# Splitting the per-head scaling of linear-attention tiles between ScalarE, VectorE and GpSimd, with one routing step moved in TensorE's order

## The chip, the cores and the metric

The kernel runs on one core of a Trainium2 chip, as one launch. The metric is device time in microseconds of that launch. A core has TensorE (PE, matmuls into PSUM), VectorE (DVE), ScalarE (ACT), GpSimd (POOL), SyncE (SP, here a queue that issues DMAs), and 16 DMA engines. Each engine works through its own instructions in their order; semaphores make them wait for each other.

## The reference, cut to what matters

Linear attention over 4 batches of 576 rows, 8 heads of 64, is followed by an RMS norm of each head, and by two mixture-of-experts layers of 8 experts over the 2304 rows of 512.

```python
kv  = einsum('bhsd,bhse->bhde', k, v)
out = einsum('bhsd,bhde->bhse', q, kv)
rms = sqrt(mean(out * out, axis=-1, keepdims=True) + 1e-06)
x   = out / rms * g_norm                 # (B,H,S,64), then rows of 512
# layer 1: rows with x @ w_skip > 0 go to expert argmax(x @ w_gate): x + gate * relu(x @ w1[e]) @ w2[e]
# layer 2: every row goes to its expert, up to a capacity: gate * relu(x @ w1[e]) @ w2[e]
```

## The kernel before, in words

The 2304 rows are 18 tiles of 128; tile numbers t0 to t17 below count them. Batch 0 fills t0 to t3 and half of t4, batch 1 ends with t8, batch 2 with half of t13.

**Attention, batch by batch.** `emit_kv` sums k·v of a batch on PE in five chunks (c0 to c4) into the PSUM tile `acc`, and ACT copies the two blocks of each head pair to `vk`. `emit_kvT` (written T) runs two filler matmuls on zeros into the PSUM tile `lg` (`warm`), transposes `vk` into the same `lg`, multiplies `vk` by the gate weights into `acc`, and ACT copies both to `kvbd`, which holds 128 columns of kv and 34 of gate weights for each head pair.

**One tile.** `emit_products(i)` multiplies q by `kvbd` into one of three PSUM tiles `ops` (pool `apo`). `emit_tile(i)` then norms it. ACT squares (`sq`), DVE sums by head (`ss`), ACT takes the root (`rm`), DVE the reciprocal (`ri`). DVE scales the 34 gate columns (`lh`) and sums them over heads to 17 logits (`Lall`). ACT copies `ops` to `og` in one instruction, POOL multiplies `og` by g_norm and then by `ri` into the row tile `xr`; 16 logits are copied behind the row, and SP writes `xr` to the table `xcat` in DRAM. For t15 alone (`G_DVE`) DVE multiplies `ops` by g_norm instead of ACT's copy and POOL's first multiply. From t16 on (`LPOOL`) POOL copies the logits. An `ops` tile can be written again when all its readers have read it.

**Routing.** After t8 the logits of the first nine tiles pick experts on DVE (`choose1`: `sel`, `oa_mx`, `oa_eq`, `oh`), a scan gives counts (`C`), PE sums them over partitions into `lg` (`R`, lines 178 and 183), and DVE makes ranks (line 196 on), one-hot matrices `As` and a table `Bt`, which PE turns into row numbers (line 796). With them POOL gathers the first 128 rows of the fullest expert (`rows`), which starts its first-layer product early (`t1`, `l1`, `l2`, lines 574, 592, 626) while the other nine tiles are ranked in the same way. The copies of that early expert's transposed rows, `xT` on line 576 and 580, are ACT's.

**Order.** PE's order is written by hand (`manual_schedule`): `ATT_SEQ` for the attention, where `t0` to `t4` are the tiles of a batch, `c0` to `c4` the chunks of the next one, `r` and `R` the two halves of the ranking, `e`, `E`, `m0`, `w` the early expert, and `EARLY_SEQ` behind it. The order on ACT, DVE and POOL is set by a scheduler from the order of the code and its own costs.

```python
ATT_SEQ = [..., "r t0 q c0 c1 t1 t2 c2 c3 R c4 t3 T", "e m0 m1 E w w p0 p1 t2 w w t3 t4"]
EARLY_SEQ = "v7 t v3 h0 h1 R h2 h3 T y0 y1 y2 y3"
```

In `EARLY_SEQ`, `v7` and `v3` are fillers, `t` the transposes of the gathered rows, `h` the first and `y` the second product of the early expert, `R` and `T` the ranking of the last nine tiles.

Of the kernel before, what the change touches and what calls it, by code (L numbers as in the profile page):

```python
# [7 lines left out]
F32 = mybir.dt.float32  # L8
# [21 lines left out]
CAP1 = [240, 176, 164, 156, 148, 144, 140, 136]  # L30
CAP2 = [384, 352, 320, 308, 300, 292, 280, 272]
EPS_G = 1e-9
LPOOL = 16
G_DVE = (15,)
EARLY_SEQ = "v7 t v3 h0 h1 R h2 h3 T y0 y1 y2 y3"
ATT_SEQ = ["t0 c0 c1 t1 t2 c2 c3 c4 t3 T", "t0 c0 c1 t1 t2 c2 c3 c4 t3 T t4", "r t0 q c0 c1 t1 t2 c2 c3 R c4 t3 T", "e m0 m1 E w w p0 p1 t2 w w t3 t4"]
KV_COL = True
SPLIT1 = (1, 2, 3, 4, 5)
AS_POOL = 0
WARM_T, LATE = 2, 100000  # L40
# [7 lines left out]
def moe_kernel(ctx: ExitStack, tc: tile.TileContext, qT, kk, vv, aux, w1a, w2a, w1b, w2b, capacity, out):  # L48
    nc = tc.nc
# [47 lines left out]
    for m, caps in ((1, CAP1), (2, CAP2)):  # L97
        t = cst.tile([1, E], F32, name=f"capc{m}")
# [23 lines left out]
    grep = au[:, 68:68 + HD]  # L122
# [13 lines left out]
    Lall = cst.tile([128, NT, 17], F32, name="Lall")  # L136
# [155 lines left out]
    m1 = first_mix.enter_context(tc.tile_pool(name="m1", bufs=1, side="right"))  # L292
# [339 lines left out]

    att = ExitStack()
    aq, asp0, asp, axp = (att.enter_context(tc.tile_pool(name=n, bufs=b)) for n, b in (("aq", 3), ("as0", 1), ("as", 3), ("ax", 12)))
    akv = att.enter_context(tc.tile_pool(name="akv", bufs=2))
    apo = att.enter_context(tc.tile_pool(name="apo", bufs=3, space=PSUM))
    with att:
        warm(p1u.tile([128, 512], F32, name="acc"), 10)
        kvbd_all, vk_all = [], []
        for i in range(2):  # L640
            kvbd_all.append(asp0.tile([128, 4, 162], F32, name=f"kvbd{i}"))
            t = asp0.tile([128, 4, 128], F32, name=f"vk{i}")
# [61 lines left out]
        def emit_kvT(b):  # L704

            vk, kb = vk_all[b % 2], kvbd_all[b % 2]
            tp = p1u.tile([128, 4, 128], F32, name="lg")
            warm(tp, WARM_T)
            for hp in range(4):
                nc.tensor.transpose(tp[:, hp, :], vk[:, hp, :], ident)  # L710
            wp = p1u.tile([128, 4, 128], F32, name="acc")
            for hp in range(4):
                nc.tensor.matmul(wp[:, hp, 0:34], lhsT=vk[:, hp, :], rhs=gw[:, hp, :], start=True, stop=True)
            with tc.high_priority():
                nc.scalar.copy(out=kb[:, :, 0:128], in_=tp)
                nc.scalar.copy(out=kb[:, :, 128:162], in_=wp[:, :, 0:34])
# [3 lines left out]
        def emit_products(i):  # L720
            t0 = i * 128
            segs = []
            o = 0
            while o < 128:
                b, s = divmod(t0 + o, S)
                n = min(128 - o, S - s)
                segs.append((o, n, b, s))
                o += n
            ps = apo.tile([128, 4, 256], F32, name="ops")
            for (o, n, b, s) in segs:  # L730
                for hp in range(4):
                    nc.tensor.matmul(ps[o:o + n, hp, 0:162], lhsT=qt[b][:, hp, s:s + n],
                                     rhs=kvbd_all[b % 2][:, hp, :], start=True, stop=True)
            PS[i] = ps

        def emit_tile(i):
            if i not in PS:
                emit_products(i)
            ps, t0 = PS[i], i * 128
            sq = asp.tile([128, 4, 128], F32, name="sq")  # L740
            nc.scalar.activation(out=sq, in_=ps[:, :, 0:128], func=AF.Square)
            ss = asp.tile([128, H], F32, name="ss")
            nc.vector.tensor_reduce(out=ss, in_=sq.rearrange("p c (h d) -> p (c h) d", h=2), axis=AX.X, op=ALU.add)
            og = asp.tile([128, H, HD], F32, name="og")
            o4, og4 = ps[:, :, 0:128].rearrange("p c (h d) -> p c h d", h=2), og.rearrange("p (c h) d -> p c h d", c=4)
            if i in G_DVE:
                nc.vector.tensor_tensor(out=og4, in0=o4, in1=grep.unsqueeze(1).unsqueeze(1).to_broadcast([128, 4, 2, HD]), op=ALU.mult)
            else:
                nc.scalar.copy(out=og4, in_=o4)
            rm = asp.tile([128, H], F32, name="rm")  # L750
            nc.scalar.activation(out=rm, in_=ss, func=AF.Sqrt, bias=eps6, scale=1.0 / HD)
            ri = asp.tile([128, H], F32, name="ri")
            nc.vector.reciprocal(out=ri, in_=rm)
            xr = axp.tile([128, ROW], F32, name="xr")
            r4 = ri.rearrange("p (c h) -> p c h", c=4).unsqueeze(3)
            lh = asp.tile([128, 4, 2, 17], F32, name="lh")
            nc.vector.tensor_tensor(out=lh, in0=ps[:, :, 128:162].rearrange("p c (h n) -> p c h n", h=2),
                                    in1=r4.to_broadcast([128, 4, 2, 17]), op=ALU.mult)
            nc.vector.tensor_reduce(out=Lall[:, i, :], in_=lh.rearrange("p c h n -> p n (c h)"), axis=AX.X, op=ALU.add)
            (nc.gpsimd.tensor_copy if i >= LPOOL else nc.scalar.copy)(out=xr[:, D:ROW], in_=Lall[:, i, 0:16])  # L760
            steps = [] if i in G_DVE else [(og, grep.unsqueeze(1))]
            steps.append((xr[:, 0:D].rearrange("p (h d) -> p h d", h=H), ri.unsqueeze(2)))
            for k, (dst, by) in enumerate(steps):
                ins = nc.gpsimd.tensor_tensor(out=dst, in0=og, in1=by.to_broadcast([128, H, HD]), op=ALU.mult)
                if "gather" in ahead and k == 0:
                    behind(ins, ahead["gather"])
            nc.sync.dma_start(out=xcat[t0:t0 + 128, :], in_=xr)

        with tc.manual_schedule(engines={mybir.EngineType.PE}):
            emit_kv(0, range(5))  # L770
            emit_kvT(0)
            def late(f):
                p = tc.cur_priority
# [34 lines left out]
            for b in range(B):  # L808
                t = list(range((b * S) // 128 if b else 0, ((b + 1) * S) // 128))
                for u in ATT_SEQ[b].split():  # L810
                    if u == "T":
                        emit_kvT(b + 1)
                    elif u == "r":
                        gen = choose_part(routed, t[0], bump1)
                        routed = t[0]
                        late(lambda: next(gen))
                    elif u == "R":
                        late(lambda: run(gen))
                        ranked = routed
# [50 lines left out]
    with first_mix:  # L870
# [11 lines left out]
        for i in range(2):  # L882
            t = cst.tile([128, NB1, E], BF16, name=f"o2_{i}")
# [541 lines left out]
```

## Time and profile before

| | |
|---|---|
| median of 3 runs | 502.59 us (501.24 to 503.12) |
| profiled execution: its own time | 502.82 us |
| its span, first to last instruction | 501.2 us |
| PE busy | 477.4 us (95%) |
| DVE busy | 303.7 us (61%) |
| ACT busy | 205.8 us (41%) |
| POOL busy | 143.3 us (29%) |

The span is 1.6 us shorter than the time of the same execution. Shares of busy time are means over attention (up to about 68 us), the early expert (to about 88 us) and the two expert layers (the rest), which differ in what limits them.

### The profile page before, as it was taken

The page shows a single profiled execution, that of the slowest core. Times are in us where ns is not written, and L with a number is a line of the kernel's source. Part 1 is how long each engine was busy: PE and PEld are TensorE (multiplying, and loading weights), DVE is VectorE, ACT ScalarE, POOL GpSimd, SP SyncE. Part 2 cuts the span into 40 slices and gives each one's busy share as a digit, 9 for nine tenths or more (in the row PEclk, how much of TensorE's full clock was granted, in tenths as well). Part 3 has the DMA queues.
Part 4 walks back from the last instruction along what each step waited for, and adds up shares of the span by engine and source line. Part 5 has one row for each costly group of instructions (what it writes and reads, how often), then busy time and mean ns, then how long its engine had stood idle before and what let it go on. Part 6 is the DMA issues. An engine that isn't in the chain of part 4 may idle for free.

```text
span 501.2 us, 10243 instructions
## 1 busy us (share of the span) xinstructions
PE 477.4 (95%) x3829; PEld 454.8 (91%) x3829; DVE 303.7 (61%) x945; ACT 205.8 (41%) x524; POOL 143.3 (29%) x179
## 2 busy tenths in 40 slices
PE   6998869799999999999999999999999999999995
PEld 3897759699999999999999799999999999999985
DVE  3167977276677665455775485664756576575711
ACT  1376541254433523113432364444555455554400
POOL 5288583101131121212125230130603215040201
PEclk8699798899999999999999999999999999999999
DMA  8999594689787776457317995465546646400001
GB/s 245 362 366 321 194 341 128 225 316 343 268 291 251 240 279 212 155 190 276 126 45 253 417 338 173 132 236 169 188 175 233 216 139 231 162 36 1 36 22 40
DMA packets 24617, 104.90 MB, mean 209 GB/s; under 512 B 3609, under 2 KB 4761, under 8 KB 15984
## 3 DMA queue, kind: packets, MB, share of 16 engines
q1 hardware_dynamic: 17264, 77.75, 44.9%
q0 software_dynamic: 7008, 26.35, 14.9%
q8 instruction: 32, 0.52, 0.4%
q14 instruction: 25, 0.20, 0.1%
q10 hardware_dynamic: 288, 0.07, 0.1%
HBM read 92.15 MB, written 12.76 MB: 209 GB/s over the span
## 4 chain that ended last, share of the span: by engine, by line
PE 75%; DVE 3%; DMA 2%; issue 1%; ACT 0%; POOL 0%; POOLq 0%; ACTq 0%
PE hp L592 14%; PE yp L1089 7%; PE yp L1091 7%; PE yp L1090 7%; PE hp L1089 6%; PE hp L1090 6%; PE hp L1091 6%; PE yp L616 6%; PE yp L626 5%; PE yp L617 2%; PE yt L1318 2%; PE tp L1274 2%; DMA wraw<-in_w1b 2%; PE tp L1011 1%; PE tp L574 1%
## 5 line engine op out<-in xcount | busy, mean ns | idle before, releaser
L979 ACT CAST whi<-wraw 128x512 fp32r<-128x512 f32 x152 | 86.1, 619 | 73.3 <-PE yp L1090 30.1
L980 DVE TENSOR_TENSOR wlo<-wraw,whi 128x512 fp32r<-128x512 f32 x152 | 97.4, 684 | 27.4 <-ACT whi L979 26.3
L592 PE MATMUL hp<-xT,wraw 128*128 128x128 f32 (+8 forms) x576 | 81.3, 300 | 3.2 <-issue 3.0
L339 POOL DMA_INDIRECT rows<-xcat,gi x40 | 42.1, 1051 | 141.5 <-ACT ex L348 88.4
L592 PEld LDWEIGHTS hp<-xT,wraw 128*128 128x128 f32 x576 | 76.6, 198 | 5.6 <-issue 4.9
L1089 PE MATMUL hp<-xh,whi 128*128 128x256 f32 (+7 forms) x256 | 78.9, 308 | 0.3 <-DVE hl L1109 0.3
L1091 PE MATMUL hp<-xh,wlo 128*128 128x256 f32 (+7 forms) x256 | 76.7, 299 | 0.0
L1090 PE MATMUL hp<-xl,whi 128*128 128x256 f32 (+7 forms) x256 | 76.6, 299 | 0.0
L1089 PE MATMUL yp<-hh,whi 128*128 128x320 f32 (+5 forms) x192 | 58.8, 306 | 0.0
L1091 PE MATMUL yp<-hh,wlo 128*128 128x320 f32 (+5 forms) x192 | 57.2, 298 | 0.0
L1090 PE MATMUL yp<-hl,whi 128*128 128x320 f32 (+5 forms) x192 | 57.2, 298 | 0.0
L1308 POOL DMA_INDIRECT out<-ot,toki x24 | 32.3, 1348 | 84.4 <-DVE su L352 39.4
L1089 PEld LDWEIGHTS hp<-xh,whi 128*128 128x128 f32 x256 | 48.2, 188 | 1.1 <-DVE hl L1109 0.8
L1090 PEld LDWEIGHTS hp<-xl,whi 128*128 128x128 f32 x256 | 48.3, 189 | 0.0
L1091 PEld LDWEIGHTS hp<-xh,wlo 128*128 128x128 f32 x256 | 48.3, 189 | 0.0
L1027 POOL DMA_INDIRECT xcat<-rows,toki x16 | 16.4, 1028 | 94.3 <-DVE mxt L297 91.8
L616 PE MATMUL yp<-hT,whi 128*128 128x352 f32 (+4 forms) x160 | 43.1, 351 | 0.0
L1108 ACT ACTIVATE hh<-hp 128x320 fp32r<-128x320 f32 (+8 forms) x64 | 27.2, 429 | 32.8 <-PE hp L1091 28.0
L1109 DVE SCALAR_TENSOR_TENSOR hl<-hp,hh 128x320 fp32r<-128x320 f32 (+8 forms) x64 | 30.0, 476 | 14.3 <-ACT hh L1108 13.1
L617 PE MATMUL yp<-hT,wlo 128*128 128x176 f32 (+4 forms) x160 | 37.7, 235 | 0.0
L1090 PEld LDWEIGHTS yp<-hl,whi 128*128 128x128 f32 x192 | 36.2, 188 | 0.0
L1089 PEld LDWEIGHTS yp<-hh,whi 128*128 128x128 f32 x192 | 36.1, 188 | 0.0
(255 smaller groups left out, 870.4 us busy)
## 6 DMA issues: line engine op xcount, KB each, us to landing
wraw<-in_w1a SPq DMA_DIRECT2D x14, 1024.0 KB
wraw<-in_w2a SPq DMA_DIRECT2D x14, 1024.0 KB
wraw<-in_w1b SPq DMA_DIRECT2D x14, 1024.0 KB
wraw<-in_w2b SPq DMA_DIRECT2D x14, 1024.0 KB
xcat<-xr SPq DMA_DIRECT2D x18, 264.0 KB
q<-in_q SPq DMA_DIRECT2D x3, 1152.0 KB
wraw<-in_k SPq DMA_DIRECT2D x6, 512.0 KB
wraw<-in_v SPq DMA_DIRECT2D x6, 512.0 KB
```

Source lines behind the costliest of these rows:

```text
L339: return nc.gpsimd.indirect_dma_start(out=rows[:n], out_offset=None, in_=xcat[0:source], in_offset=bass.IndirectOffsetOnAxis(ap=gi[:n], ax ...
L592: nc.tensor.matmul(hp[:, ff, :], lhsT=wv[:, fc % 4, k, :], rhs=XT[j][:, k, c0:c1], start=(k == 0), stop=(k == 3))
L616: nc.tensor.matmul(yp, lhsT=wh[:, fc, :], rhs=HT[j][:, fc], start=(fc == 0), stop=False, skip_group_check=True)
L617: nc.tensor.matmul(yp[:, 0, :], lhsT=wl[:, fc, :], rhs=HT[j][:, fc, 0, :], start=False, stop=(fc == 7), skip_group_check=True)
L979: nc.scalar.copy(out=hi[:, cs], in_=raw[:, cs])
L980: ins = nc.vector.tensor_tensor(out=lo[:, cs], in0=raw[:, cs], in1=hi[:, cs].bitcast(F32), op=ALU.subtract)
L1089: nc.tensor.matmul(ps, lhsT=wh, rhs=xh, start=first, stop=False)
L1090: nc.tensor.matmul(ps, lhsT=wh, rhs=xl, start=False, stop=False)
L1091: nc.tensor.matmul(ps, lhsT=wl, rhs=xh, start=False, stop=last)
L1108: ea = nc.scalar.activation(out=hh[:, fs, cs], in_=hp, func=AF.Relu)
L1109: ev = nc.vector.scalar_tensor_tensor(out=hl[:, fs, cs], in0=hp, scalar=0.0, in1=hh[:, fs, cs].bitcast(F32), op0=ALU.max, op1=ALU.subtract)
L1308: st = nc.gpsimd.indirect_dma_start(out=out, out_offset=bass.IndirectOffsetOnAxis(ap=r2["toki"][:nn, j, bi:bi + 1], axis=0), in_=ot[:nn], ...
```

## The change

- Each tile has a kind (`KINDS`). In a **B** tile (t0, t1, t2, t4, t5, t6, t8, t9, t11, t12, t14, t15) ACT scales each of the 8 heads by its column of `ri`, in 8 instructions of 128x64 from `ops` to `og`, in place of one copy of 128x512, and POOL multiplies once, by g_norm. In a **D** tile (t3, t7, t10, t13, t16) DVE multiplies `ops` by g_norm and POOL multiplies once, by `ri`; ACT copies nothing. In the one **A** tile (t17) DVE multiplies by g_norm, ACT scales the 8 heads, and POOL does nothing.
- `LPOOL = 99`: ACT copies the logits of all tiles.
- In batch 2's sequence `R` comes behind `c4 t3` and not ahead of them.
- `emit_kvT` runs its two fillers for batch 0 alone, so 3 pairs go.
- `og` has a pool of 5 buffers of its own, where it had 3. `sq`, `lh` and the g_norm product are written with the even heads first; sizes stay.

```diff
-LPOOL = 16
-G_DVE = (15,)
+LPOOL = 99
+KINDS = "BBBDBBBDBBDBBDBBDA"
...
-"r t0 q c0 c1 t1 t2 c2 c3 R c4 t3 T"
+"r t0 q c0 c1 t1 t2 c2 c3 c4 t3 R T"
...
+    aog = att.enter_context(tc.tile_pool(name="aog", bufs=5))
...
-            warm(tp, WARM_T)
+            if b == 0:
+                warm(tp, WARM_T)
...
-            og = asp.tile([128, H, HD], F32, name="og")
-            if i in G_DVE:
-                nc.vector.tensor_tensor(out=og4, in0=o4, in1=grep.unsqueeze(1).unsqueeze(1).to_broadcast([128, 4, 2, HD]), op=ALU.mult)
-            else:
-                nc.scalar.copy(out=og4, in_=o4)
...
+            og = aog.tile([128, H, HD], F32, name="og")
+            kind = KINDS[i]
+            if kind in "DA":
+
+                nc.vector.tensor_tensor(out=byparity(og), in0=o4, in1=grep.unsqueeze(1).unsqueeze(1).to_broadcast([128, 2, 4, HD]), op=ALU.mult)
+            if kind in "BA":
+
+                for h in range(H):
+                    src, dst = (ps[:, h // 2, (h % 2) * HD:(h % 2) * HD + HD], og) if kind == "B" else (og[:, h, :], x3)
+                    nc.scalar.activation(out=dst[:, h, :], in_=src, func=AF.Copy, scale=ri[:, h:h + 1])
...
-            steps = [] if i in G_DVE else [(og, grep.unsqueeze(1))]
-            steps.append((xr[:, 0:D].rearrange("p (h d) -> p h d", h=H), ri.unsqueeze(2)))
...
+            steps = {"P": [(og, grep.unsqueeze(1)), (x3, ri.unsqueeze(2))], "D": [(x3, ri.unsqueeze(2))],
+                     "B": [(x3, grep.unsqueeze(1))], "A": []}[kind]
```

Three places show what the scheduler and the hand-written order make of it. First ACT around t3 and t4, before: `sq_436` is t3's square and `sq_477` t4's, each with its copy to `og` next to it.

```order
L741 ACTIVATE sq_436<-ops_431 128x512
L749 COPY og_440<-ops_431 128x512
L715 COPY kvbd1_199<-lg_454 128x4x128
L716 COPY kvbd1_199<-acc_461 128x4x34
L751 ACTIVATE rm_442<-ss_438,eps6_123 128x8
L741 ACTIVATE sq_477<-ops_468 128x512
L760 COPY xr_446<-Lall_146 128x16
L749 COPY og_481<-ops_468 128x512
L751 ACTIVATE rm_483<-ss_479,eps6_123 128x8
```

The same place on ACT with the change; `sq_457`, `rm_461` and `xr_466` are t3's (a D tile), `sq_495` and `og_503` t4's, `sq_541` is t5's.

```order
L746 ACTIVATE sq_457<-ops_452 128x2x4x64
L746 ACTIVATE sq_495<-ops_486 128x2x4x64
L750 ACTIVATE rm_461<-ss_459,eps6_123 128x8
L750 ACTIVATE rm_499<-ss_497,eps6_123 128x8
L769 COPY xr_466<-Lall_146 128x16
L768 ACTIVATE og_503<-ops_486,ri_501 128x64 x8
L769 COPY xr_504<-Lall_146 128x16
L746 ACTIVATE sq_541<-ops_536 128x2x4x64
```

t4's reads of `ops` now stand behind both roots and behind the copy of t3's logits, where before they stood next to its square; the next squares stand behind t4's eight heads.

Second, ACT at the end of the attention. Before, from t17's square (`sq_984`) to the copies of the early expert's rows:

```order
L741 ACTIVATE sq_984<-ops_979 128x512
L760 COPY xr_945<-Lall_146 128x16
L751 ACTIVATE rm_967<-ss_963,eps6_123 128x8
L749 COPY og_988<-ops_979 128x512
L751 ACTIVATE rm_990<-ss_986,eps6_123 128x8
L576 COPY xT1_1039<-tp1_1040 128x2x128
L580 COPY xT1_1039<-tp1_1044 128x2x128
```

With the change, from t15's heads (`og_1002`) on; `sq_1049` is t17's square, `rm_1031` and `xr_1036` are t16's.

```order
L768 ACTIVATE og_1002<-ops_989,ri_1000 128x64 x8
L769 COPY xr_1003<-Lall_146 128x16
L750 ACTIVATE rm_1031<-ss_1029,eps6_123 128x8
L746 ACTIVATE sq_1049<-ops_1044 128x2x4x64
L769 COPY xr_1036<-Lall_146 128x16
L750 ACTIVATE rm_1053<-ss_1051,eps6_123 128x8
L768 ACTIVATE xr_1058<-og_1057,ri_1055 128x64 x8
L769 COPY xr_1058<-Lall_146 128x16
L576 COPY xT1_1111<-tp1_1112 128x2x128
L580 COPY xT1_1111<-tp1_1116 128x2x128
```

The copies of the early expert's rows stood behind t17's root and now stand behind its eight heads and its logits too.

Third, PE at the end of batch 2, with the change, from the last chunks on:

```order
L699 MATMUL acc<-wraw 64x64 x16
L699 MATMUL acc<-k_252,v_253 64x64 x8
L734 MATMUL ops<-kvbd_199,q_248 128x162 x4
L178 LDWEIGHTS ones
L178 MATMUL lg<-C_0_695,ones 128x72
L183 LDWEIGHTS ntri
L183 MATMUL lg<-oh_0_685,ntri 128x72
L712 MATMUL lg<-ident,vk_203 128x128 x4
```

The ranks' product into `lg` stood ahead of `c4` and t12's product and is now behind them, right ahead of the transposes, which write the same `lg` (before, a product and two fillers lay between).

## Rows read from the trace of the kernel before

**Rows 1.** The page's first line, and windows: stretch, length, then busy time by engine.

```profile
span 501.2 us, 10243 instructions
17.50:50.00 32.50, 30.28 (x379) 27.85 (x380) 19.71 (x55) 20.62 (x57) 24.77 (x23) 0.92 1.03 344
50.00:75.00 25.00, 19.39 (x127) 16.29 (x125) 21.43 (x68) 12.61 (x32) 17.12 (x19) 0.88 0.73 266
```

**Rows 2.** Timeline of PE, 27 to 81 us: start, us, instruction, [idle before it].

```profile
27.36 0.59 PE L111 MATMUL lg<-zb 128*128 128x512 bf16 x2
27.79 0.60 PE L710 MATMUL lg<-ident,vk 128*128 128x128 f32 x4
...
48.09 0.19 PE L178 MATMUL lg<-C,ones 128*128 128x72 bf16 x1 [1.72 <-DVE C L173]
...
67.67 0.63 PE L574 MATMUL tp<-ident,rows 128*128 128x128 f32 x4 [1.69 <-DVE ri L753]
...
68.78 3.76 PE L592 MATMUL hp<-xT,wraw 128*128 128x128 f32 x32
74.37 0.21 PE L178 MATMUL lg<-C,ones 128*128 128x72 bf16 x1 [1.83 <-DVE C L173]
...
75.11 5.44 PE L592 MATMUL hp<-xT,wraw 128*128 128x128 f32 x32
80.38 0.38 PE L856 MATMUL acc<-Bt,As 128*128 128x32 bf16 x9
```

**Rows 3.** Timeline of ACT, 20 to 69 us.

```profile
20.39 0.60 ACT L741 ACTIVATE sq<-ops 128x512 f32<-128x512 f32 x1 [2.62 <-PE ops L732]
...
21.75 0.30 ACT L751 ACTIVATE rm<-ss,eps 128x8 f32<-128x8 f32 x1 [0.28 <-DVE ss L743]
...
24.56 0.60 ACT L741 ACTIVATE sq<-ops 128x512 f32<-128x512 f32 x1
25.05 0.29 ACT L751 ACTIVATE rm<-ss,eps 128x8 f32<-128x8 f32 x1
25.25 0.58 ACT L749 COPY og<-ops 128x512 f32<-128x512 f32 x1
...
26.32 0.37 ACT L701 COPY vk<-acc 64x256 f32<-64x256 f32 x1
...
39.14 0.61 ACT L715 COPY kvbd<-lg 128x512 f32<-128x512 f32 x1
39.62 0.30 ACT L716 COPY kvbd<-acc 128x136 f32<-128x136 f32 x1
39.78 0.33 ACT L751 ACTIVATE rm<-ss,eps 128x8 f32<-128x8 f32 x1
...
41.28 0.20 ACT L760 COPY xr<-Lall 128x16 f32<-128x16 f32 x1
41.39 0.58 ACT L749 COPY og<-ops 128x512 f32<-128x512 f32 x1
...
68.11 0.37 ACT L576 COPY xT<-tp 128x256 f32<-128x256 f32 x1 [0.29 <-PE tp L574]
```

**Rows 4.** Timeline of DVE: t0's four steps, t15's product with g_norm, the late `sel`.

```profile
21.02 0.69 DVE L743 TENSOR_REDUCE ss<-sq 128x8 f32<-128x512 f32 x1 [12.12 <-ACT sq L741]
22.08 0.20 DVE L753 RECIPROCAL ri<-rm 128x8 f32<-128x8 f32 x1 [0.37 <-ACT rm L751]
22.39 0.30 DVE L757 TENSOR_TENSOR lh<-ops,ri 128x136 f32<-128x136 f32 x1
22.72 0.39 DVE L759 TENSOR_REDUCE Lall<-lh 128x17 f32<-128x136 f32 x1
...
62.95 0.68 DVE L747 TENSOR_TENSOR og<-ops,au 128x512 f32<-128x512 f32 x1
...
69.08 3.19 DVE L676 TENSOR_SCALAR sel<-Lall 128x9 f32<-128x9 f32 x1
```

**Rows 5.** Timeline of POOL, its last multiply of the attention (t17's).

```profile
71.20 1.03 POOL L764 TENSOR_TENSOR xr<-og,ri 128x512 f32<-128x512 f32 x1
```

More of the change, by code (lines that the diff above doesn't have):

```diff
@@ L32 @@
 EPS_G = 1e-9
-LPOOL = 16
-G_DVE = (15,)
+LPOOL = 99
+KINDS = "BBBDBBBDBBDBBDBBDA"
 EARLY_SEQ = "v7 t v3 h0 h1 R h2 h3 T y0 y1 y2 y3"
-ATT_SEQ = ["t0 c0 c1 t1 t2 c2 c3 c4 t3 T", "t0 c0 c1 t1 t2 c2 c3 c4 t3 T t4", "r t0 q c0 c1 t1 t2 c2 c3 R c4 t3 T", "e m0 m1 E w w p0 p1 t2 w w t3 t4"]
+ATT_SEQ = ["t0 c0 c1 t1 t2 c2 c3 c4 t3 T", "t0 c0 c1 t1 t2 c2 c3 c4 t3 T t4", "r t0 q c0 c1 t1 t2 c2 c3 c4 t3 R T", "e m0 m1 E w w p0 p1 t2 w w t3 t4"]
 KV_COL = True
@@ L739, in emit_tile @@
             ps, t0 = PS[i], i * 128
-            sq = asp.tile([128, 4, 128], F32, name="sq")
-            nc.scalar.activation(out=sq, in_=ps[:, :, 0:128], func=AF.Square)
-            ss = asp.tile([128, H], F32, name="ss")
-            nc.vector.tensor_reduce(out=ss, in_=sq.rearrange("p c (h d) -> p (c h) d", h=2), axis=AX.X, op=ALU.add)
-            og = asp.tile([128, H, HD], F32, name="og")
-            o4, og4 = ps[:, :, 0:128].rearrange("p c (h d) -> p c h d", h=2), og.rearrange("p (c h) d -> p c h d", c=4)
-            if i in G_DVE:
-                nc.vector.tensor_tensor(out=og4, in0=o4, in1=grep.unsqueeze(1).unsqueeze(1).to_broadcast([128, 4, 2, HD]), op=ALU.mult)
-            else:
-                nc.scalar.copy(out=og4, in_=o4)
+            byparity = lambda t: t.rearrange("p (c a) d -> p a c d", a=2)
+            o4 = ps[:, :, 0:128].rearrange("p c (a d) -> p a c d", a=2)
+            g4 = ps[:, :, 128:162].rearrange("p c (a n) -> p a c n", a=2)
+            sq = asp.tile([128, H, HD], F32, name="sq")
+            nc.scalar.activation(out=byparity(sq), in_=o4, func=AF.Square)
+            ss = asp.tile([128, H], F32, name="ss")
+            nc.vector.tensor_reduce(out=ss, in_=sq, axis=AX.X, op=ALU.add)
             rm = asp.tile([128, H], F32, name="rm")
@@ L753, in emit_tile @@
             nc.vector.reciprocal(out=ri, in_=rm)
+            og = aog.tile([128, H, HD], F32, name="og")
             xr = axp.tile([128, ROW], F32, name="xr")
[L755 to L759, printed above, removed]
+            x3 = xr[:, 0:D].rearrange("p (h d) -> p h d", h=H)
+            lh = asp.tile([128, 2, 4, 17], F32, name="lh")
+            nc.vector.tensor_tensor(out=lh, in0=g4, in1=ri.rearrange("p (c a) -> p a c", a=2).unsqueeze(3).to_broadcast([128, 2, 4, 17]),
+                                    op=ALU.mult)
+            nc.vector.tensor_reduce(out=Lall[:, i, :], in_=lh.rearrange("p a c n -> p n (a c)"), axis=AX.X, op=ALU.add)
+            kind = KINDS[i]
[5 more added lines that the diff above has]
+                    nc.scalar.activation(out=dst[:, h, :], in_=src, func=AF.Copy, scale=ri[:, h:h + 1])
             (nc.gpsimd.tensor_copy if i >= LPOOL else nc.scalar.copy)(out=xr[:, D:ROW], in_=Lall[:, i, 0:16])
-            steps = [] if i in G_DVE else [(og, grep.unsqueeze(1))]
-            steps.append((xr[:, 0:D].rearrange("p (h d) -> p h d", h=H), ri.unsqueeze(2)))
+            if kind == "P":
+                nc.scalar.copy(out=byparity(og), in_=o4)
+            steps = {"P": [(og, grep.unsqueeze(1)), (x3, ri.unsqueeze(2))], "D": [(x3, ri.unsqueeze(2))],
+                     "B": [(x3, grep.unsqueeze(1))], "A": []}[kind]
             for k, (dst, by) in enumerate(steps):
```

## The prediction

> **What bounds the kernel now.** The windows come first [rows 1]: from 17.5 to 50 us PE is busy for 30.28 of 32.50 us and ACT for 20.62, so PE sets the pace there and ACT has some 12 us of slack. From 50 to 75 us PE has 5.6 us of gaps. The timeline of PE shows which gaps matter [rows 2]: 1.72 us ahead of the first ranks (waiting for `C`), 1.69 us ahead of the early expert's transposes, 1.83 us ahead of the second ranks (again `C`). After the last of these, 32 matmuls take 5.44 us where the same 32 took 3.76 us before it: the granted clock fell to the lower level for part of them, 1.68 us lost. From 80.4 us on PE is nearly always busy and nothing is edited, so I carry a shift at that place to the end of the span undiminished.
>
> The timeline of ACT gives the price list [rows 3], read from start to start, since ACT begins an instruction about 0.1 us before the last one's busy time ends. A square takes 0.49 us (24.56 to 25.05), a root 0.20 (25.05 to 25.25), a copy of 16 logits 0.11 (41.28 to 41.39); for one batch `vk` takes twice 0.37, `kvbd` 0.48 and 0.16, together 1.38. ACT's turn for the early rows, `xT`, comes at 68.11, and the first product of the early expert starts 0.67 us later, at 68.78 [rows 2, 3].
>
> **The price of one head.** No row shows a copy of 64 columns with a column as scale. From below: a copy of 16 costs 0.11; the square's other 496 elements cost 0.38, 0.77 ns each, so 64 plain elements cost 0.15. From above: a root of 8 elements, which takes a column as its bias, costs 0.20, and 56 elements more (0.04) make 0.24. The root is nearer: it too reads an operand per partition, and the copy of 16 doesn't. I take 0.24, and keep 0.15 to 0.24 for the range. Eight heads are then 1.92 us, where the one copy took about 0.5.
>
> The Trainium skill (ScalarE: Activation LUTs, What ACT_TABLE_LOAD costs) gives 186 ns + 0.833 ns per element, 93 ns more for each pointer operand and 93 ns of overlap back to back; by it a head is an estimated 0.24 us as well, and the sum below stays as it is. No run here shows it for a scale.
>
> **ACT's new work.** A B or A tile costs 0.49 + 0.20 + 1.92 + 0.11 = 2.72 us, a D tile 0.80. 12 B, one A and 5 D make 35.4 + 4.0, and three batches of kv copies 4.1: 43.5 us between t0's square at 20.39 [rows 3] and the `xT` copies, which now stand behind all of it. Before, there were 47.7 us for this (20.39 to 68.11). If ACT never waited, it would be done 4.2 us earlier than now. But ACT works strictly in its order, and the new order makes it wait for DVE.
>
> **ACT's waits.** One tile's chain is, from the start of its square: `ss` 0.63 later and 0.69 long, then `rm`, `ri` at 1.69 to 1.89 [rows 3, 4], so no head before 1.92. For t0 ACT has only a square and a root to fill these 1.92: 1.2 idle. For t1 and t2 two squares and two roots (1.38) stand against 2.16: 0.8 idle. With t3 and t4, the copy of t3's logits stands ahead of t4's heads: after t4's root at 2.16, DVE still does t3's `ri`, `lh`, product with g_norm and `Lall` (0.20, 0.30, 0.68 and 0.39 [rows 4], partly overlapped with the root), to about 3.35: 1.2 more, 2.0 in all. In the same way: 0.4 at t5 and t6 (the `vk` copies fill the rest), 1.9 at t7 to t9 (t7's logits again), 1.4 at t10 to t12, 2.5 at t13 and t14 (behind the first nine tiles' one-hots on DVE). At the end nothing fills: t16's root and t17's square, then t16's DVE chain to its logits (1.2 idle), then `ss` of t17 (0.5), root, `ri`, `lh`, product (1.3): 3.0. Sum 13.2 us.
>
> PE can't run ahead of this, since `ops` has three buffers and a B tile's is free only after its eighth head: t8's product waits for t5's heads, t11's for t8's, and so on. PE's own work in the stretch, some 30 us of 32.5, fits into ACT's pauses, so the pace is ACT's.
>
> So `xT` starts at 20.39 + 43.5 + 13.2 = 77.1, 9.0 us late. What waits behind it is PE's first early product, and all behind that.
>
> **What the other parts give.** The fillers' three pairs cost PE 0.43 us each (27.36 to 27.79 [rows 2]), 1.3 us in all; it now waits for ACT there, so I count nothing. If PE were the bound they would count in full. `c4` and t12's product fill the 1.72 us wait for `C`, but the transposes behind the ranks write the same `lg` and must wait for DVE's first read of it, which DVE reaches only after t12's `ss`, behind t12's square on ACT. Hidden behind ACT too, so nothing; 1.72 us where PE is the bound.
>
> POOL loses half its multiplies. It wasn't the bound, but `sel` took 3.19 us and ended at 72.27, just when t17's multiply on POOL ended (72.23) [rows 4, 5], where other small DVE steps take 0.2 to 0.4. t17 now has no multiply there, so `sel` should be short and `C` ready about 7 us after t15's last head, ahead of the end of the early expert's first two products. The wait of 1.83 us therefore goes: −1.83. The low clock behind it I leave in the sum: PE now idles some 4 us before the early products, longer than the 1.83 us that preceded the drop in before, so the same 1.68 us are lost one product earlier (bounds: 1.68 less to 1.68 more, if two drops come).
>
> The larger DMAs move with the rows they wait for. The early weights stand on SP behind t12's write, and the gather of the early rows waits for the first nine tiles' row numbers on DVE, both behind t12's heads by the same reckoning; the transposes stood at 67.67 [rows 2], and even 5 us later they would still be ahead of the new `xT` turn. I count nothing.
>
> **Sum.** +9.0 − 1.83 = +7.2 us. Against the profiled execution's own 502.82 us that is 510.0; that execution lies 0.2 us above the median of 502.59, on which it makes **509.8 us**.
>
> **Rivals.** (A) PE stays the bound and the routing gets shorter: **faster**. Then the first wait for `C` (1.72), the fillers (1.3), the second wait (1.83) and the drop behind it (1.68) all go: −6.5, 496.1 us. It decides at an `xT` of 69.9 (68.11 + 1.83): earlier is a gain, that is with heads under 0.17 us and the waits as reckoned, or with heads of 0.24 and waits under 6.0 us in place of 13.2. With heads at the lower bound of 0.15, 104 of them save 9.4 us, `xT` comes at 67.7, and the two last terms go with it: −3.9, 498.7. For it speaks `sel`; against it the root's 0.20.
>
> The Trainium skill (SBUF — State Buffer, Who interferes with whom) has GpSimd and VectorE share a port pair that the first holds for its whole instruction while the other fully blocks; by that rule fewer POOL multiplies shorten DVE's chains and the change is a gain of the size of A. The trace agrees with the rule for `sel`, at 3.19 us [rows 4]; it doesn't say that this chain stays the last.
>
> (B) The order's waits are half as long, because DVE, freed of POOL, answers sooner: 6.6 us, `xT` at 70.5, +2.4 − 1.83 = +0.6: 503.2, no change.
>
> (C) The clock falls often, with PE idle in short gaps and no fillers: the transposes (0.60 us [rows 2]) and the products of `vk`, about as long, lie between two ACT steps in three batches, and at the lower level they take twice as long: 1.2 us each, +3.6, 513.4 us.
>
> **Chances.** The forecast 0.60 (506 to 512), C 0.06, B 0.14, A 0.20. A range of 499 to 514 holds C and leaves out A's better end. Within 0.5% (500.1 to 505.1, about what a measurement of this kernel can tell from no change) lies B: 0.14; below it A: 0.20; above it the rest: 0.66.
>
> **What would show it.** Right: eight-head groups of about 1.9 us; ACT over 75% busy from 20 to 70 us, with PE gaps there that end on ACT's heads (readers of `ops`); `xT` near 77; `sel` short; no wait for `C` ahead of the second ranks. Wrong: heads near 0.15 us from start to start, PE still full from 20 to 46 us, or squares that run while heads wait, so that `xT` comes before 70. The step that I trust least is the sum of the waits, since it is reckoned tile by tile and not read from a row.

## The result, and the profile after

The changed kernel takes 509.83 us (median of 4 runs, 508.12 to 511.21), the kernel before 502.86 us on the same chip (4 runs, 501.24 to 503.66): a ratio of 1.0141 [1.0095, 1.0188], 7.0 us slower. The profiled execution took 508.65 us, its span is 506.9 us.

The windows of the changed kernel, with the columns of [rows 1]:

```profile
17.50:50.00 32.50, 26.11 (x312) 23.18 (x312) 15.56 (x47) 23.39 (x92) 9.80 (x8) 0.95 0.99 324
50.00:75.00 25.00, 19.07 (x145) 15.63 (x146) 19.22 (x68) 17.78 (x71) 12.36 (x11) 0.80 0.62 220
```

PE was busy for 30.28 us of the first window and is now for 26.11, with 312 matmuls in place of 379: it has lost its hold on the pace. ACT is 72% busy (23.39 of 32.50), POOL down from 24.77 to 9.80. No engine is full: that is a chain of engines that wait for one another. The timeline of PE names the waits, as in [rows 2]:

```profile
27.72 0.76 PE L712 MATMUL lg<-ident,vk 128*128 128x128 f32 x4 [0.84 <-ACT vk L703]
...
42.27 1.37 PE L734 MATMUL ops<-kvbd,q 128*128 128x162 f32 x8 [1.29 <-ACT og L768]
...
47.96 1.37 PE L734 MATMUL ops<-kvbd,q 128*128 128x162 f32 x8 [1.50 <-DVE og L763]
...
57.45 0.63 PE L712 MATMUL lg<-ident,vk 128*128 128x128 f32 x4 [2.72 <-DVE rk L196]
...
74.62 0.97 PE L574 MATMUL tp<-ident,rows 128*128 128x128 f32 x4
...
78.55 5.46 PE L592 MATMUL hp<-xT,wraw 128*128 128x128 f32 x32 [2.31 <-ACT xT L576]
83.86 0.20 PE L178 MATMUL lg<-C,ones 128*128 128x72 bf16 x1
...
84.58 3.81 PE L592 MATMUL hp<-xT,wraw 128*128 128x128 f32 x32
88.23 0.38 PE L867 MATMUL acc<-Bt,As 128*128 128x32 bf16 x9
88.46 7.39 PE L626 MATMUL yp<-hT,wraw 128*128 128x128 f32 x64
```

Products into `ops` wait for ACT's last head (L768) or, behind a D tile, for DVE's product (L763). The first early product stands at 78.55 us, where it stood at 68.78 [rows 2], and waits for ACT's `xT`. Behind it the second ranks (83.86) wait for nothing, where they waited 1.83 us. The low clock has moved one product ahead, as its two groups of 32 show: 5.46 and 3.81 us now, 3.76 and 5.44 before. The windows with the columns of [rows 1] have the granted clock (the third number from the end, 0.50 for the lower level), before and after:

```profile
77.00:79.50 2.50, 2.50 (x14) 2.50 (x13) 1.45 (x10) 0.39 (x1) 0.00 (x0) 0.50 0.12 47
...
79.00:82.00 3.00, 3.00 (x16) 3.00 (x16) 0.00 (x0) 1.27 (x2) 0.00 (x0) 0.50 0.93 289
```

The products of `Bt` and `As` into `acc` were at 80.38 and are at 88.23.

The timeline of ACT, t0's tile and then t17's, as in [rows 3]:

```profile
20.10 0.60 ACT L746 ACTIVATE sq<-ops 128x512 f32<-128x512 f32 x1 [2.62 <-PE ops L734]
21.45 0.30 ACT L750 ACTIVATE rm<-ss,eps 128x8 f32<-128x8 f32 x1 [0.75 <-DVE ss L748]
22.43 1.75 ACT L768 ACTIVATE og<-ops,ri 128x64 f32<-128x64 f32 x8 [0.68 <-DVE lh L757]
24.02 0.25 ACT L769 COPY xr<-Lall 128x16 f32<-128x16 f32 x1
...
76.12 2.02 ACT L768 ACTIVATE xr<-og,ri 128x64 f32<-128x64 f32 x8 [1.27 <-DVE og L763]
78.05 0.19 ACT L769 COPY xr<-Lall 128x16 f32<-128x16 f32 x1
78.14 0.36 ACT L576 COPY xT<-tp 128x256 f32<-128x256 f32 x1
```

Eight heads that read PSUM (`ops`) take 1.59 us from start to start (22.43 to 24.02), 0.20 each; t17's, which read `og` in SBUF, 1.93 (76.12 to 78.05), 0.24 each. ACT's groups by line, from t0's square to `xT` (20.10 to 78.14): busy time and mean ns, then the idle time ahead and what ended it.

```profile
L768 ACT ACTIVATE og<-ops,ri 128x64 f32<-128x64 f32 x96 | 21.4, 343 | 2.9 <-DVE lh L757 2.7
L746 ACT ACTIVATE sq<-ops 128x512 f32<-128x512 f32 x18 | 10.8, 656 | 3.6 <-PE ops L734 3.6
L750 ACT ACTIVATE rm<-ss,eps 128x8 f32<-128x8 f32 x18 | 5.3, 305 | 3.9 <-DVE ss L748 3.8
L769 ACT COPY xr<-Lall 128x16 f32<-128x16 f32 x18 | 4.3, 241 | 4.8 <-DVE Lall L759 4.8
L768 ACT ACTIVATE xr<-og,ri 128x64 f32<-128x64 f32 x8 | 2.0, 334 | 1.3 <-DVE og L763 1.3
...
L702 ACT COPY vk<-acc 64x256 f32<-64x256 f32 x3 | 1.1, 357 | 0.3 <-PE acc L699 0.3
L718 ACT COPY kvbd<-acc 128x136 f32<-128x136 f32 x3 | 0.9, 288 | 0.6 <-PE lg L796 0.6
```

The idle times add up to 17.4 us, 12.6 of them ended by DVE. But 2.62 of the 3.6 us that PE ended lie ahead of t0's square, so ahead of the stretch; within it ACT is idle for 14.8 us, and busy for the other 43.2 of 58.04, as the second of these windows has it:

```profile
20.00:70.00 50.00, 37.72 (x435) 33.64 (x435) 31.61 (x106) 38.10 (x148) 19.17 (x17) 0.94 0.80 266
20.10:78.14 58.04, 43.86 (x454) 37.18 (x454) 37.61 (x124) 43.20 (x170) 22.16 (x19) 0.91 0.83 278
```

An idle time counts from the end of the busy time before it. The prediction prices from start to start, which leaves the last 0.1 us or so of each instruction ahead of a wait to the wait. By such prices the heads cost 96 × 0.199 + 8 × 0.241 = 21.0 us and the rest, as the prediction had it, 18.5: an estimate of 39.5 us of work, which leaves 18.5 us for the waits.

The late `sel` on DVE, the answer to [rows 4]:

```profile
76.41 0.17 DVE L677 TENSOR_SCALAR sel<-Lall 128x9 f32<-128x9 f32 x1
...
78.32 0.31 DVE L173 TENSOR_TENSOR_SCAN C<-smask,oh 128x72 bf16<-128x72 f32 x1
```

It takes 0.17 us where it took 3.19, and `C` is there 5 us ahead of the ranks that need it. POOL's last multiply is t16's and ends at 74.82, ahead of it.

### The profile page after: what moved, and what is told of

It reads as the page before. It is cut to its first block, busy times and chain, and to the rows that moved or that the text cites. A ratio compares the mean times of both kernels' runs of the same rounds, so it can differ in the third digit from the quotient of the medians.

```text
span 506.9 us, 10284 instructions
## 1 busy us (share of the span) xinstructions
PE 476.7 (94%) x3823; PEld 452.1 (89%) x3823; DVE 300.2 (59%) x950; ACT 219.0 (43%) x613; POOL 126.4 (25%) x159
## 4 chain that ended last, share of the span: by engine, by line
PE 73%; DVE 3%; DMA 2%; issue 1%; ACT 0%; POOL 0%; POOLq 0%; ACTq 0%
PE hp L592 13%; PE yp L1100 7%; PE yp L1102 7%; PE yp L1101 7%; PE hp L1100 6%; PE hp L1101 6%; PE hp L1102 6%; PE yp L616 6%; PE yp L626 4%; PE yp L617 2%; PE yt L1329 2%; PE tp L1285 2%; DMA wraw<-in_w1b 2%; PE tp L1022 1%; PE tp L574 1%
## 5 line engine op out<-in xcount | busy, mean ns | idle before, releaser
L592 PE MATMUL hp<-xT,wraw 128*128 128x128 f32 (+8 forms) x576 | 79.9, 296 | 4.8 <-ACT xT L576 2.5
L592 PEld LDWEIGHTS hp<-xT,wraw 128*128 128x128 f32 x576 | 75.1, 194 | 7.4 <-issue 4.2
L1319 POOL DMA_INDIRECT out<-ot,toki x24 | 34.1, 1422 | 84.8 <-DVE su L352 39.4
L734 PE MATMUL ops<-kvbd,q 128*128 128x162 f32 (+1 forms) x160 | 28.9, 343 | 8.6 <-ACT og L768 4.3
```

The source lines that it names most:

```text
L592: nc.tensor.matmul(hp[:, ff, :], lhsT=wv[:, fc % 4, k, :], rhs=XT[j][:, k, c0:c1], start=(k == 0), stop=(k == 3))
L1319: st = nc.gpsimd.indirect_dma_start(out=out, out_offset=bass.IndirectOffsetOnAxis(ap=r2["toki"][:nn, j, bi:bi + 1], axis=0), in_=ot[:nn], ...
```

## The experiments

Twelve kernels ran, with their ratios to the kernel before on the same chip. Theory 1 (later called H): the heads on ACT, with the waits in ACT's strict order, set the pace and cost the time. Theory 2, for e1 to e8: the other edits, or the order alone, do. For e9 to e12 the rival was theory E: only the end counts, where t17's heads stand ahead of `xT`. A tile of kind P has one copy on ACT and two multiplies on POOL, as most tiles have before the change. The table puts together where the PE timeline of each places four steps (us): the last batch's transposes, the fillers behind t17's product, the first early product (L592) and its second-layer product (L626). The steps are those of one profiled execution, the medians those of all; e6, whose rows come out otherwise, stands apart.

| kernel | transposes | fillers | L592 | L626 | median us | ratio [95%] |
|---|---|---|---|---|---|---|
| before | 51.79 | 64.30 | 68.78 | 80.61 | 502.86 | |
| the change | 57.45 | 71.63 | 78.55 | 88.46 | 509.83 | 1.0141 [1.0095, 1.0188] |
| e1_plain_copy | 51.06 | 68.63 | 72.98 | 82.04 | 502.75 | 1.0024 [0.9999, 1.0049] |
| e2_all_dve | 53.59 | 70.55 | 76.17 | 86.07 | 507.50 | 1.0129 [1.0088, 1.0170] |
| e3_ranks_moved | 51.33 | 67.14 | 71.12 | 81.47 | 499.70 | 0.9954 [0.9908, 1.0000] |
| e4_no_fillers | 50.98 | 66.54 | 70.90 | 82.78 | 502.83 | 1.0018 [0.9992, 1.0043] |
| e5_ranks_back | 57.14 | 71.76 | 78.59 | 88.75 | 509.51 | 1.0148 [1.0067, 1.0229] |
| e7_half_heads | 54.94 | 70.67 | 77.02 | 88.05 | 507.67 | 1.0122 [1.0054, 1.0190] |
| e8_end_only | 53.07 | 69.81 | 76.80 | 87.46 | 510.68 | 1.0179 [1.0108, 1.0250] |
| e9_end_as_before | 58.62 | 73.31 | 77.03 | 86.11 | 507.84 | 1.0144 [1.0086, 1.0202] |
| e10_end_late_heads | 52.60 | 69.26 | 74.63 | 84.30 | 506.51 | 1.0116 [1.0053, 1.0179] |
| e11_late_heads_both | 53.24 | 69.96 | 74.58 | 84.45 | 505.27 | 1.0112 [1.0072, 1.0151] |
| e12_change_late_heads | 58.68 | 73.34 | 78.21 | 86.49 | 507.82 | 1.0139 [1.0078, 1.0199] |

The column L626 orders the kernels nearly as their medians do: from this step to the median it is 418.2 to 423.2 us, so what has reached it is carried to the end, give or take some 2.5 us.

**e1_plain_copy: the changed kernel, no heads.** t15 keeps DVE's product as before; all other tiles are of kind P. The ranks' place, the fillers, the pool and the logits copies stay changed.

```diff
-KINDS = "BBBDBBBDBBDBBDBBDA"
+KINDS = "PPPPPPPPPPPPPPPDPP"
```

> Theory 1 (ACT's queue of eight heads and the waits in it set the pace): with one copy per tile and two POOL multiplies again, and the ranks' move, the missing fillers and the logits' copies as changed, ACT's work falls by some 17 us to about 27, the early rows' copy on ACT comes at 66 to 70 us as in before, and the time is 497 to 504. Theory 2 (the missing fillers or the moved ranks cost the time): they are still in, so the time stays within 2 us of the changed kernel's 509.8.

502.75 us, 1.0024: the kinds cost the time, the rest together nearly nothing. The time is theory 1's; `xT` isn't where it was expected (66 to 70 us), but at 72.56.

**e2_all_dve: every tile on DVE.**

```diff
-KINDS = "BBBDBBBDBBDBBDBBDA"
+KINDS = "DDDDDDDDDDDDDDDDDD"
```

> All tiles of kind D: no heads on ACT, 12 more products with g_norm on DVE (0.68 us each, some 9 us more DVE work), one POOL multiply a tile. Theory 1: ACT isn't the bound, its early rows' copy comes ahead of 70 us, and with the shorter waits for the ranks the time is 496 to 503. Theory 2: 508 or more. A third reading, that a D tile's own chain on DVE (the logits behind the product) is what holds ACT, gives 503 to 508.

507.50 us with not one head on ACT, which is the third reading's range. So the number of heads is not the whole story: all 18 products on DVE (0.68 us each [rows 4], 12.2 us) cost nearly as much.

**e3_ranks_moved and e4_no_fillers: one part alone, in the kernel before.**

```diff
-"r t0 q c0 c1 t1 t2 c2 c3 R c4 t3 T"
+"r t0 q c0 c1 t1 t2 c2 c3 c4 t3 R T"
```

> The kernel before with the ranks' product behind the last chunk and the last tile's product, and nothing else. Theory 1: the wait of 1.72 us for C is filled, but the transposes now wait for DVE's read of the same PSUM tile; within 2 us of the 502.9 of before. Theory 2 (the move is what costs): 505 or more.

```diff
-            warm(tp, WARM_T)
+            if b == 0:
+                warm(tp, WARM_T)
```

> The kernel before with the fillers of batches 1 to 3 left out, and nothing else. Theory 1: PE is the bound there, so up to 1.3 us less, 501 to 503. Theory 2 (without them the clock falls more often): 505 or more, with more stretches at the lower level between 25 and 70 us.

0.9954 [0.9908, 1.0000] and 1.0018 [0.9992, 1.0043]: neither costs time; the ranks' new place may even gain a little. Theory 2 in its first form falls.

**e5_ranks_back: the changed kernel with the ranks at their old place.**

```diff
-"r t0 q c0 c1 t1 t2 c2 c3 c4 t3 R T"
+"r t0 q c0 c1 t1 t2 c2 c3 R c4 t3 T"
```

> The changed kernel with the ranks' product back ahead of the last chunk. Theory 1 (ACT's queue sets the pace up to the last transposes): PE waits for ACT there anyway, so the time stays within 2 us of 509.8, though the transposes no longer wait for DVE's read behind the ranks. Theory 2, as the all-D kernel and the moved ranks alone suggest (the transposes there wait 2.7 to 4.0 us for that read): 505 to 507.5.

509.51 us, transposes at 57.14: as with the change. The wait of 2.72 us for `rk` ahead of the transposes is not what costs; they are late with it and without it.

**e6_no_pointer: heads without a column as scale.**

```diff
-nc.scalar.activation(out=dst[:, h, :], in_=src, func=AF.Copy, scale=ri[:, h:h + 1])
+nc.scalar.activation(out=dst[:, h, :], in_=src, func=AF.Copy, scale=1.0)
```

> The changed kernel with the heads' scale by a fixed 1.0 in place of the column of ri: the scaling by 1/rms is left out of the rows in B tiles and in the last tile. A head is then 0.11 to 0.15 us from start to start, where it is 0.20. Theory 1: ACT has 5 to 9 us less to do, the early rows' copy comes at 71 to 74 us and the time is 503 to 506. Theory 2: within 2 us of 509.8.

591.53 us. This kernel leaves out the scaling by 1/rms, so its rows go on unscaled and only the attention can be compared. The timeline of ACT, t0:

```profile
22.43 1.04 ACT L768 ACTIVATE og<-ops 128x64 f32<-128x64 f32 x8 [0.68 <-DVE lh L757]
23.27 0.28 ACT L769 COPY xr<-Lall 128x16 f32<-128x16 f32 x1
```

Eight heads in 0.84 us, 0.105 each, in place of 0.20: the column costs 0.094 us per head. The last batch's transposes come at 54.08, 3.4 us ahead of the change, `xT` at 73.91, as theory 1 had it, and the first early product at 74.33, 4.2 ahead. The instructions are as many; ACT's order differs in places (in t1 and t2 the `kvbd` copies stand behind other heads), and a head no longer reads `ri`, though t0's still starts at 22.43. So the length of the heads counts up to there; of the nearly 10 us that the 104 heads are shorter, 4.2 arrive.

**e7_half_heads: P in place of half the B tiles.**

```diff
+KINDS = "BPBDPBPDBPDBPDBPDA"
```

> The changed kernel with five of the twelve B tiles (t1, t5, t8, t11, t15) back to one copy on ACT and two multiplies on POOL. Theory 1: each B tile that goes gives ACT 1.1 us back, 5.5 us in all, so 503.5 to 506.5. Theory 2 (order and waits decide, not the number of heads): within 2 us of 509.8.

Six B tiles became P (t1, t4, t6, t9, t12, t15), not the five that the expectation names. 507.67 us: the transposes gain 2.5 us, L626 only 0.4. Theory 1 as I had put it fails, since six tiles less should have given back more than its 5.5 us. The medians differ by 2.2 us, the ratios by 0.0019, and the intervals overlap: nothing shows a gain beyond doubt.

**e8_end_only: the changed kernel, heads in t17 alone, fillers back.**

```diff
-KINDS = "BBBDBBBDBBDBBDBBDA"
+KINDS = "PPPPPPPPPPPPPPPDDA"
...
-            if b == 0:
-                warm(tp, WARM_T)
+            warm(tp, WARM_T)
```

> One copy and two POOL multiplies for t0 to t14, the kinds D, D and A for the last three tiles, the ranks moved, the fillers back. Theory 1: ACT isn't the bound up to t14; at the end sel is short and the wait for C ahead of the second ranks (1.83 us) goes, against eight heads (1.6 us) ahead of the early rows' copy: 499 to 503. Theory 2: as the one-copy kernel, 502 to 504.

510.68 us, which neither theory had: as slow as the whole change, though t0 to t16 have no heads. It differs from e1 in t16, t17 and the fillers. PE at the early product:

```profile
76.80 6.23 PE L592 MATMUL hp<-xT,wraw 128*128 128x128 f32 x32 [4.24 <-ACT xT L576]
82.86 0.20 PE L178 MATMUL lg<-C,ones 128*128 128x72 bf16 x1
```

PE idles for 4.24 us, and the 32 matmuls behind take 6.23 us where [rows 2] has 3.76. This made theory E. Not all of the loss is the end's: the transposes already come 2.0 us later than in e1, the fillers behind t17's product 1.2 us.

**e9_end_as_before: the other half.** t0 to t14 keep their kinds; t15 to t17 are multiplied as before the change (ACT still copies their logits).

```diff
-KINDS = "BBBDBBBDBBDBBDBBDA"
+KINDS = "BBBDBBBDBBDBBDBDPP"
```

> The changed kernel with its last three tiles as they were before the change (t15: VectorE multiplies by g_norm; t16 and t17: one plain ScalarE copy and two GpSimd multiplies), so that no head stands between the last tiles and the xT copies; t0 to t14 keep their heads. Theory H (the heads on ScalarE along the whole attention are the price): transposes of the last batch near 57.4 us as with the change, fillers after t17 near 71, first early product near 75.5, second-ranks wait back (+1.9), total 507 to 511 us. Theory E (the end chain alone is the price: t16's logits, t17's product on VectorE and eight heads ahead of the xT copies, and the low clock that follows the idle): first early product 4.4 us behind the fillers in place of 6.9, no clock drop behind it, total 502 to 505 us.

507.84 us, a ratio of 1.0144: theory H, and E falls as the only cause. But its steps are half of each: the early product 3.7 us behind the fillers, with no drop behind it, as E had it, and yet late, since the fillers come at 73.31. PE there:

```profile
58.62 0.63 PE L712 MATMUL lg<-ident,vk 128*128 128x128 f32 x4 [2.72 <-DVE rk L196]
...
64.73 0.38 PE L807 MATMUL acc<-Bt,As 128*128 128x32 bf16 x9
...
77.03 3.84 PE L592 MATMUL hp<-xT,wraw 128*128 128x128 f32 x32 [0.43 <-ACT xT L576]
```

And in e1, with no heads:

```profile
51.06 1.11 PE L712 MATMUL lg<-ident,vk 128*128 128x128 f32 x4 [2.78 <-ACT vk L703]
...
60.51 0.19 PE L807 MATMUL acc<-Bt,As 128*128 128x32 bf16 x1 [1.35 <-DVE As L218]
61.57 0.21 PE L807 MATMUL acc<-Bt,As 128*128 128x32 bf16 x1 [0.88 <-DVE As L218]
62.02 0.70 PE L807 MATMUL acc<-Bt,As 128*128 128x32 bf16 x4 [0.24 <-DVE As L218]
```

In e1 PE reaches the products of `As` early and waits for DVE's one-hots one by one; in e9, 7.6 us late at the transposes, it finds all nine ready. So a part of the delay by heads is swallowed by a wait that was there anyway: 7.56 us at the transposes are 4.05 at L592 (77.03 − 72.98). The profiled execution of e9 also has the clock at its lower level from 43.0 to 46.4 us, which the change's doesn't have; its transposes come 1.2 us later than the change's.

**e10_end_late_heads: e8 with t17's heads behind `xT` on ACT.**

```diff
-                    nc.scalar.activation(out=dst[:, h, :], in_=src, func=AF.Copy, scale=ri[:, h:h + 1])
+                    ins = nc.scalar.activation(out=dst[:, h, :], in_=src, func=AF.Copy, scale=ri[:, h:h + 1])
+                    if i >= 16:
+                        HEADS.append(ins)
...
-                        t1(0, 0, 128, nc.scalar.copy)
+                        def evac(**kw):
+                            last = nc.scalar.copy(**kw)
+                            for ins in HEADS:
+                                behind(ins, last)
+                        t1(0, 0, 128, evac)
```

> The kernel of the run with changed ends only (510.7 us), with t17's eight heads ordered behind the two xT copies on ScalarE; same work, other order. Theory E: the xT copies come 1.6 us (eight heads of 0.2) to 3 us (with the waits of the first head) sooner than 76.4 us, the first early product runs at full clock, total 503 to 506 us. Theory H, or that the D and A tiles cost through VectorE's products: xT no more than 1 us sooner, total 508 to 511 us.

506.51 us, 4.2 less than e8 by the medians, nearer to E; the ratios' intervals still overlap (1.0116 to e8's 1.0179). ACT and PE there:

```profile
74.10 0.20 ACT L771 COPY xr<-Lall 128x16 f32<-128x16 f32 x1 [1.19 <-DVE Lall L759]
74.21 0.36 ACT L576 COPY xT<-tp 128x256 f32<-128x256 f32 x1
74.48 0.38 ACT L862 COPY xT<-tp 128x256 f32<-128x256 f32 x1
74.74 2.02 ACT L768 ACTIVATE xr<-og,ri 128x64 f32<-128x64 f32 x8
```

```profile
74.63 5.23 PE L592 MATMUL hp<-xT,wraw 128*128 128x128 f32 x32 [2.62 <-ACT xT L576]
```

`xT` starts 2.17 us sooner (76.38 in e8). The drop expected to go does not: PE still idles for 2.62 us, and the 32 matmuls take 5.23 us. What stands ahead of `xT` on ACT is now t17's logits copy, which waits for DVE.

**e11_late_heads_both: e10 with t16 like t17.**

```diff
-KINDS = "PPPPPPPPPPPPPPPDDA"
+KINDS = "PPPPPPPPPPPPPPPDAA"
```

> As the run before in this call, and t16 too is multiplied on VectorE alone and gets its eight heads on ScalarE behind the xT copies; GpSimd multiplies neither t16 nor t17. Theory E: like the run before in this call or up to 3 us faster, since VectorE's one-hot chain meets no GpSimd multiply (2.2 us from sel to C in place of 5.1) and the second ranks do not wait: total 498 to 505 us. If VectorE's two products in the last chain cost more than that (0.68 us each): 505 to 511 us.

505.27 us, just in the second range that was expected, its interval within that of e10. `sel` was short in e10 already (0.17 us), so there was nothing left to gain there. With neither POOL multiply in the way this is still 1.1% slower than before.

**e12_change_late_heads: the change with e10's edit.**

> The changed kernel with t17's eight heads ordered behind the two xT copies on ScalarE, nothing else. Theory H: total 508 to 510 us, 1 to 2 us less than the change at most. Theory E: first early product from 78.6 to 75.5 to 76.5 us, the clock drop behind the idle gone (1.6 us), total 504 to 507 us.

507.82 us, a ratio of 1.0139, which can't be told from the change's 1.0141. By the time it is nearest to H. The early product comes 4.9 us behind the fillers, 2.0 sooner than with the change, and its 32 matmuls take 3.84 us, without the drop, as E had it; but the fillers came 1.7 us later in this execution (granted clock at its lower level from 43.3 to 46.7 us as well, which the change's execution doesn't have).

No kernel beat the one before beyond doubt; e3, at 0.9954 with an interval that ends at 1, came nearest.

## Why the prediction was right

**ACT's queue: right in kind, two terms mis-sized with opposite signs.** ACT at 76% busy from 20 to 70 us (38.10 of 50.00), PE's waits for readers of `ops`, the short `sel` and the ranks without a wait are all as the prediction's signs had them; the eight heads out of PSUM, at 1.59 us, are shorter than its 1.9. `xT` was forecast at 77.1 and starts at 78.14. The head was taken at 0.24 us and costs 0.20 for the 96 that read PSUM; only t17's eight cost 0.24. By the prediction's own prices ACT's work is thus 39.5 us and not 43.5. The waits, the step that I trusted least, are 18.5 us and not 13.2: each group of tiles waits longer than reckoned, t10 to t12 most. These take 10.69 us, from t10's square to t13's:

```profile
51.86 1.21 ACT L746 ACTIVATE sq<-ops 128x512 f32<-128x512 f32 x2
...
62.55 0.66 ACT L746 ACTIVATE sq<-ops 128x512 f32<-128x512 f32 x1
```

Their work is 6.9 us, so they wait for 3.8, where 1.4 were reckoned. The reckoning let a first head start behind `ri`, at 1.92 us from the square; the trace has it behind `lh`, for t0 at 2.33 (20.10 to 22.43). It had no wait of a square for PE either (1.0 us in the stretch). t0's square starts 0.3 us sooner; −0.3, −4.0 and +5.3 make the +1.0, so the forecast of `xT` is better than its terms. That the median lies within 0.1 us of the forecast is luck on top of a right mechanism: these terms cancel, and the four runs of the change are 3.1 us apart.

The Trainium skill (ScalarE: Activation LUTs, What ACT_TABLE_LOAD costs), by which a head was an estimated 0.24 us, agrees with t17's heads out of SBUF (0.24) and with the price of the column (93 ns there, 0.094 us between e6 and the change); heads out of PSUM were 0.04 us shorter.

**The second ranks: right.** `sel` is short, `C` is early, the wait of 1.83 us is gone. **The low clock: right as a net of nothing.** The same loss lies one product earlier (5.46 + 3.81 against 3.76 + 5.44 us). From L592 (+9.77) to L626 (+7.85) the shift shrinks by 1.92; forecast were −1.83, and a sum of +7.2.

**Nothing for fillers, ranks and DMAs: right,** by e4, e3 and e5 for the first two. As for the DMAs, the transposes of the gathered rows came at 74.62, 7.0 us later than before, more than the 5 that I allowed, and still ahead of ACT's turn for `xT`.

**"Carried to the end undiminished": off by 2.4 us in the profiled pair.** From L626 to the next ranks the kernel before needs 17.27 us (80.61 to 97.88), the changed one 14.89 (88.46 to 103.35). Before:

```profile
89.45 1.15 PE L592 MATMUL hp<-xT,wraw 128*128 128x112 f32 x8 [0.22 <-ACT xT L576]
93.59 4.39 PE L592 MATMUL hp<-xT,wraw 128*128 128x112 f32 x24 [3.00 <-issue]
```

After:

```profile
97.24 1.59 PE L592 MATMUL hp<-xT,wraw 128*128 128x112 f32 x12 [0.23 <-ACT xT L576]
101.07 2.38 PE L592 MATMUL hp<-xT,wraw 128*128 128x112 f32 x20 [2.25 <-issue]
```

Before, a pause of 3.00 us is followed by a stretch at the lower level (93.5 to 96.9 us) and 0.18 us per matmul; after, the pause is 2.25 us, the clock stays at its upper level, 0.12 each. In e8 the pause is 2.75 us and the low level is back (98.9 to 105.7). The pause alone doesn't decide it, as e4 and then e12 show at the same place:

```profile
95.39 3.94 PE L592 MATMUL hp<-xT,wraw 128*128 128x112 f32 x20 [2.25 <-issue]
...
99.65 2.38 PE L592 MATMUL hp<-xT,wraw 128*128 128x112 f32 x20 [2.78 <-issue]
```

e4 has the change's 2.25 us and a drop (95.3 to 98.7), e12 2.78 and none. The medians differ by 7.0 us, the profiled pair by 5.8. The four runs of the change lie at 508.1, 508.7, 511.0 and 511.2, with mean granted clocks of 0.970, 0.975, 0.967 and 0.964, which would fit a drop in some executions only; that is argued, not shown, since one execution alone was profiled.

**The rivals.** A fell: PE is not full up to 50 us and `xT` comes 8 us past its point of 69.9, though `sel` did what it spoke for. B fell: the waits are 14.8 us by the profile's idle times and 18.5 by the prediction's prices, not 6.6. C fell: the transposes take 0.63 to 0.76 us and not 1.2, and from 45 to 100 us the clock stands at its lower level for 13.7 us in both executions, before in four stretches of 3.4 us, after in two of 3.4 and one of 6.9 (68.5 to 75.4). C's price was a little low: the products of `vk` are not about as long as the transposes, the pair takes 1.34 us from start to start before (27.79 to 29.13), so +4.0 and not +3.6.

**What the prediction did not see.** It made one queue of ACT's work the cause. The experiments show two that are each enough: heads along t0 to t14 (e9, +1.4%) and the end of t16 and t17 (e8, +1.8%), together no more than either (+1.4%). At L626, measured from e1, e9 is 4.07 us late, e8 5.42, the change 6.42; the low stretches lie elsewhere in each of these executions, and e8 has the fillers, which e1 lacks. Fillers behind the moved ranks cost nothing in e3, but with the tiles of before. A late start of the last batch is partly swallowed by the wait for one-hots (e1, e9). What stays open: why e10 and e11, without heads ahead of `xT`, are still 1.1% behind the kernel before. Their early products wait 2.62 and 1.88 us for `xT`, which stands behind a logits copy that waits for DVE (its products for t16 and t17), low stretches fall on these products (74.2 to 77.6 and 74.9 to 78.3 us) and again between 95 and 102 us, and the fillers are back; which of these weighs what was not separated. Nor is it shown why DVE's one-hots end some 3 us later in e1, e3 and e4 (As products done at 61.9 to 62.7 us) than in the kernel before (59.38).

## What to carry to other kernels

Splitting one wide instruction into eight narrow ones on an engine with slack uses the slack up; price the narrow ones from start to start, and then reckon the waits of an engine that works strictly in its order, naming for each group what releases its first instruction. Before moving work to shorten one chain, look at what stands behind it on the engine that takes the work, here the copies that feed the next stage. And when a loss seems found, test both halves of the change alone: two causes can each be enough, so that mending one gives nothing back.

## What the runs showed of the hardware

A 128x64 activation with a column as scale took 0.20 us from start to start out of PSUM and 0.24 out of SBUF (sixteen of e11's in 3.83 us); without the column, 0.105 out of PSUM and 0.147 out of SBUF (t17's eight in e6, 72.64 to 73.82). So the column cost 0.094 us with either source, and PSUM as the source was 0.04 us shorter with or without it. e11, then e6:

```profile
74.04 3.93 ACT L768 ACTIVATE xr<-og,ri 128x64 f32<-128x64 f32 x16
77.87 0.20 ACT L771 COPY xr<-Lall 128x16 f32<-128x16 f32 x1
...
72.64 1.28 ACT L768 ACTIVATE xr<-og 128x64 f32<-128x64 f32 x8 [0.91 <-DVE og L763]
73.82 0.19 ACT L769 COPY xr<-Lall 128x16 f32<-128x16 f32 x1
```

The tiny `sel` on DVE took 3.19 us while POOL multiplied and 0.17 when it didn't, which agrees with the Trainium skill (SBUF — State Buffer, Who interferes with whom): the engine that comes second on the shared port pair waits for the first's whole instruction. In e9 it was one such instruction: `sel` took 0.98 us and ended at 77.07, POOL's multiply at 77.04. In the kernel before it was a row of them: none of POOL's instructions there is longer than 1.3 us, and `sel` ended (72.27) with the last multiply of the row (72.23).
